# Two transformer layers on one core: the last score pairs over three PSUM tiles, a projection's tail among the first w1 groups, and w2 with the low part first

## The chip, the core and the metric

The kernel runs on one core of a Trainium2 chip. Its engines work in parallel, each through its own instruction stream: TensorE (PE, matmul; its weight loads are listed apart as PEld), VectorE (DVE), ScalarE (ACT), GpSimd (POOL) and SyncE (SP, which here only issues DMAs). Matmul results land in PSUM, eight banks of 512 fp32 columns on 128 partitions. The metric is device time in microseconds (us) of one execution; lower is better.

## The reference

Two identical layers over x of shape 1 x 2048 x 512, with the same weights in both:

```python
x = x + attention(layernorm(x), wqkv, wo)      # 32 heads of 16
x = x + mish_mlp(layernorm(x), w1, b1, w2)     # hidden 1792
x = x + attention(layernorm(x), wqkv, wo)
x = x + mish_mlp(layernorm(x), w1, b1, w2)
```

Attention is `softmax(q k^T / 4) v` over all 2048 keys, then a 512 x 512 projection wo. The MLP is `h = x w1 + b1`, `h * tanh(softplus(h))`, then w2. Everything is fp32.

## The kernel before, in words

**Precision.** Dense products (qkv, wo, w1, w2) are made from fp32r operands split in a high and a low part: `mm3` (L176) issues three matmuls per 128-row block (high x high, high x low, low x high). The p times v products are fp32.

**Tiling.** The sequence is cut in four chunks of 512 queries and sixteen key tiles of 128; heads go in eight groups of four. A *step* is one (group, chunk, key tile): 4 heads x 128 keys x 512 queries; there are 512 steps in a layer, and 16 steps make a *block*.

**Attention** needs the row maximum before the exponential. `max_mm` (L363) computes scores a first time (PSUM tag `mx`, two tiles of two banks) and DVE reduces them (L387); after 16 max steps `max_fold` (L391) folds the block's maxima, POOL splits them, and eight DMAs on SP's queue take them through DRAM (`nd`) into two extra rows of `qs`. With those rows the second computation of the scores comes out with the maximum subtracted. It is done three heads at a time: `pair` (L422) makes two heads into one two-bank tile `sp` and ACT takes the exponential (L432), `single` (L434) makes the third into a one-bank tile `ss` (L442). `pv` (L444) multiplies older p tiles with v into the accumulator `pv` (tag `acc`, one bank), and `drain` copies a finished block out. In L41 to L53, the string `CYCLE` gives the order within a step: P pair, S single, M max, v pv.

Max steps run ahead of the scores by `AHEAD` = 24 steps. The first `AHEAD + PRE` = 28 of them are put between groups of the q/k/v projections, by `some_max` in `qkv` (L538): twelve behind q/k groups and one behind every third group of three matmuls of the v projection. The first 2 x `PRE` M places of the loop go to the v projection of the last chunk (`v_parts`, L598), whose PSUM pairs share the tag `mx`. So the last 24 steps of the loop, and the four after them that hold only pv, have no maxima.

**PSUM.** Tag `mx` 2 x 2 banks, `acc` one bank, and during the loop `s2` (the pair) two banks and `s1` (the single) one: eight in all. Outside the loop the last three are three banks of tag `s`.

**After attention.** `HeadsOut` divides by the softmax sums: it loads numerators and sums from DRAM (`num`, `den`), inverts (DVE, L643), spreads the reciprocal by DMA (`rec`, POOL's queue), multiplies, and splits in `oh`, `ol`. `wo_parts` (L665) projects: sixteen groups of three matmuls a chunk, and an addition into the residual x2 (L685) after each half. In the loop's last 16 steps one group of projection 0 is issued at each step's end (`FILL`, generator `fill`). Projections 1 and 2 follow the loop, with the layer norm of chunk 0 (`norm_parts`) between their groups. Projection 3 is done in quarters within the MLP.

**MLP.** `hid(c, f)` (L690) is a w1 group of twelve matmuls and the Mish chain on ACT and DVE: hb (L701), min, exp, ..., the high part ah (L711) and then the low part al (L712). `outp(c, f)` (L715) is a w2 group of twelve matmuls into four banks; it follows `hid` by `LAG` = 2 groups, first ah with w2's two parts, then al with w2's high part. Norms of later chunks (`norm_blocks`, L266; statistics in L183) are spread over the groups by hooks.

**Buffers.** Most SBUF tiles come from the pool `blk`: 22 buffers of 8 KB per partition for everything from p tiles to weights, num, rec, oh and ol; a tile waits until a buffer comes free.

**What sets the order.** PE's order is the program's, by a chain of order-only dependencies (`pe`, L314). The other engines' instructions are ordered by a planner with a cost model, so ready work may be issued ahead of its place in the program; `behind` (L117) pins an instruction behind the one traced before it on the same engine.

Of the kernel before, what the change touches and what calls it, by code (L numbers as in the profile page):

```python
# [9 lines left out]
F32 = mybir.dt.float32  # L10
# [29 lines left out]
TR = 32  # L40
AHEAD = 24  # L41
PRE = 4
FILL = 12
KEEP = 2
# [4 lines left out]
HEADS = STEPS * HG  # L49
LAG = 2  # L50
MAX_M = (6, 3, 7)
T_BUFS = {"he": 1, "hr": 1}
# [16 lines left out]
def kernel(ctx: ExitStack, tc: tile.TileContext, x, wqkv, wo, w1, b1, w2, out):  # L69
# [113 lines left out]
    def statistics(src, nm):  # L183
        st = tmp.tile([P, NCH, 6], F32, tag="st", name=f"st{nm}")
        mv = tmp.tile([P, NCH, 2], F32, tag="mv", name=f"mv{nm}")
        ve = tmp.tile([P, NCH], F32, tag="ve", name=f"ve{nm}")
        rs = tmp.tile([P, NCH], F32, tag="rs", name=f"rs{nm}")
        for t in range(NCH):
            nc.vector.bn_stats(st[:, t], src[:, t])
            nc.vector.bn_aggr(mv[:, t], st[:, t])  # L190
        nc.gpsimd.tensor_scalar(ve, mv[:, :, 1], EPS, None, op0=ALU.add)
        nc.gpsimd.tensor_tensor(rs, ve, mhalf, op=ALU.pow)
        return rs, mv
# [110 lines left out]
    class Attention:  # L304
        def __init__(self, l, scr):
            self.l, self.scr = l, scr
            self.vscr = dram.tile([NG, P, NKT, HG * VW], F32, name=f"vscr{l}")
            self.oscr = [dram.tile([KT, 2, P, CW], F32, name=f"oscr{l}{c}") for c in range(NCH)]
            self.va = {}
            self.qk, self.mxs, self.pts, self.accs = {}, {}, [], {}  # L310
            self.singles, self.full, self.unit = 0, None, 0
            self.chained, self.last = False, None

# [49 lines left out]
        def max_mm(self, s, half):  # L363
            if s >= STEPS:
                return
            b, i = divmod(s, NKT)
# [55 lines left out]
        def pair(self):  # L422
            i = 3 * len(self.pts)
            n = min(2, HEADS - i)
            if n <= 0:
                return
            sp = self.pool.tile([P, 2, CW], F32, tag="s2", name=f"sp{self.l}{i}")
            self.pts.append(b8([P, 3, CW], F32, f"p{self.l}{i}"))
            for e in range(n):
                k, q = self.head_rows(i + e)  # L430
                self.pe(nc.tensor.matmul(sp[:, e], k, q, start=True, stop=True))  # L431
            nc.scalar.activation(self.pts[-1][:, 0:n], sp[:, 0:n], AF.Exp, scale=SCALE)  # L432
# [49 lines left out]

        def run(self, hooks, pre, fill):
            self.prep_v(0, range(NCH - 1))
            left = 2 * PRE
            close_banks()
            with tc.tile_pool(name="sa", bufs=1, space=PSUM, reuse_waits="tile") as self.pool:
                half, done = 2 * (AHEAD + PRE), -4
                for s in range(STEPS + 4):
                    if s % GSTEPS == GSTEPS - NKT and s // GSTEPS + 1 < NG:  # L490
                        self.prep_v(s // GSTEPS + 1)
                    for item in CYCLE[s % 3]:
# [15 lines left out]
                        else:  # L508
                            done += 1
                            self.pv(units(done))  # L510
                    if s + FILL >= STEPS:
                        next(fill, None)
                    for fn in hooks.get(s, []):
# [20 lines left out]
    def qkv(l, att, wts, tt, order, within, due):  # L534
# [57 lines left out]
        for c in range(NCH - 1):  # L592
            for _ in v_parts(l, c, wts, tt, att, False):
                i += 1
                if i % 3 == 0:
                    some_max()
# [68 lines left out]
    def wo_parts(l, c, outs, wot, x2, pe, paired=True):  # L665
        oh, ol = outs[c].out
        for t in range(NCH):
# [15 lines left out]
            if paired and t % 2:  # L683
                x2v = x2[:, t - 1 : t + 1]
                behind(nc.vector.tensor_tensor(x2v, acc, x2v, op=ALU.add))  # L685

    def mlp(l, x2s, w1t, w2t, tts, dst, hooks, pe):
        acts, obs = {}, {}
# [26 lines left out]
        def outp(c, f):  # L715
# [3 lines left out]
            w = w2t[f // 2]  # L719
            terms = [[(t, act, part) for t in range(NCH)] for act, part in ((ah, 0), (ah, 1), (al, 0))]  # L720
            turns = zip(*terms) if f == FT - 1 else [terms[0] + terms[1], terms[2]]
            for t, act, part in (x for turn in turns for x in turn):
                pe(
                    nc.tensor.matmul(  # L724
                        obs[c][t // 2][:, t % 2],
                        act[:, ts(t, P)],
                        w[:, part, f % 2],
                        start=f == part == 0 and act is ah,
                        stop=f == FT - 1 and act is al,
                    )  # L730
                )
# [9 lines left out]
        for i in range(len(seq) + LAG):  # L741
            if i < len(seq):
                c, f = seq[i]
                hid(c, f)
                for fn in hooks.get((c, f), []):
                    fn()
# [50 lines left out]
    for l in range(2):  # L797
# [58 lines left out]

        fill = project(0)
        att.run(hooks, v_parts(l, NCH - 1, wts, tt, att, True), fill)
        outs[3].load()
# [39 lines left out]
        if l == 0:  # L899
            last = NCH - 1  # L900
            for f, js in ((2, (0,)), (4, (2,)), (9, (1,)), (11, (3,)), (12, (4,)), (13, (5,))):
                hooks.setdefault((last, f), []).append(lambda js=js: load_qkv(1, wts, js, splits))
            for c in range(last):
                spread(hooks, last, (1, 5, 8)[c], x2s[c], f"q1{c}", tt, c)
        mlp(l, x2s, w1t, w2t, tts, xs if l == 0 else out, hooks, att.pe)
    close_banks()

# [27 lines left out]
```

## Time and profile before

| | us |
|---|---|
| median of 3 runs | 3534.33 (3533.1 to 3535.59) |
| the profiled execution | 3532.86 |
| its span | 3531.1 |
| PE busy | 3512.9 (99%) |
| DVE busy | 3002.7 (85%) |
| ACT busy | 2582.8 (73%) |
| POOL busy | 239.2 (7%) |

The profile is of one execution; its times are us from the first instruction. Rows of a timeline read: start, duration, engine, line, operation, output<-input tiles, shape (for PE rows x columns of the weights, then the output), count, and in brackets how long the engine sat idle before and what released it. Names drop buffer numbers: `mo` is a w2 accumulator, `h` a w1 one, `wo`, `va`, `vp` those of the projections, `pm` the scores for the maxima. The ends of matmuls are modelled: a stretched matmul can hide a wait. The granted clock of TensorE (PEclk) is 0.999 over the run.

### The profile page before, as it was taken

To read this page: it belongs to the slowest core of one execution; us is meant where nothing else is said; L and a number is where in the kernel's file an instruction comes from. 1 tells how busy PE (TensorE), PEld (TensorE's weight loads), DVE (VectorE), ACT (ScalarE), POOL (GpSimd) and SP (SyncE) were. 2 spreads that over 40 slices of the span, in tenths; PEclk is the share of its full clock that TensorE was granted. 3 is DMA by queue.
4 is the path that set the end of the run, shared out by engine and by line. 5 is a ranking of instruction groups with operands and counts; after the bars stand their busy time and mean duration, and the time that the engine had idled before them with its cause. 6 is when DMAs were issued, how large, how long until landed. Compare 5 with 4: busy or idle time off the path is not lost.

```text
span 3531.1 us, 68820 instructions
## 1 busy us (share of the span) xinstructions
PE 3512.9 (99%) x28572; PEld 1922.5 (54%) x28572; DVE 3002.7 (85%) x3160; ACT 2582.8 (73%) x3513; POOL 239.2 (7%) x392
## 2 busy tenths in 40 slices
PE   9999999999999999999999999999999999999999
PEld 7644444444444444788876444444444444447887
DVE  6789999999999994776756999999999999947665
ACT  3288888888888888356622888888888888874665
POOL 3100001010000002100010000000000000021000
PEclk9999999999999999999999999999999999999999
DMA  7641312213131124630364211112121111247100
GB/s 250 228 92 47 83 47 74 61 51 71 43 81 42 49 81 71 207 96 25 111 217 147 48 39 38 38 29 44 31 36 39 41 36 31 79 74 222 66 13 24
DMA packets 182196, 273.97 MB, mean 78 GB/s; under 512 B 67508, under 2 KB 111476, under 8 KB 168060
## 3 DMA queue, kind: packets, MB, share of 16 engines
q1 hardware_dynamic: 154964, 192.91, 21.4%
q10 hardware_dynamic: 19176, 43.06, 3.5%
q0 software_dynamic: 7744, 33.60, 3.4%
q8 instruction: 224, 3.67, 0.4%
q14 instruction: 88, 0.72, 0.1%
HBM read 158.87 MB, written 109.58 MB: 76 GB/s over the span
## 4 chain that ended last, share of the span: by engine, by line
PE 96%; DVE 2%; DMA 1%; issue 1%; ACT 0%; POOL 0%; SPq 0%; DVEq 0%; ACTq 0%; POOLq 0%
PE pv L457 30%; PE pm L383 18%; PE ss L441 13%; PE sp L431 10%; PE mo L724 8%; PE h L179 3%; PE h L181 3%; PE h L180 3%; PE qk L179 2%; PE qk L180 1%; PE qk L181 1%; PE wo L179 1%; PE va L179 1%; PE wo L181 1%; PE wo L180 1%
## 5 line engine op out<-in xcount | busy, mean ns | idle before, releaser
L387 DVE TENSOR_REDUCE mxv<-pm 128x2 f32<-128x1024 f32 x2048 | 2385.2, 1219 | 138.6 <-PE pm L383 88.5
L432 ACT ACTIVATE p<-sp 128x1024 f32<-128x1024 f32 x1366 | 1395.9, 1022 | 19.7 <-PE sp L431 15.3
L457 PE MATMUL pv<-p,va 128*32 128x256 f32 (+2 forms) x16032 | 1166.9, 392 | 0.1
L383 PE MATMUL pm<-ks,qs 48*128 48x512 f32 x4096 | 1096.0, 446 | 0.3
L442 ACT ACTIVATE p<-ss 128x512 f32<-128x512 f32 x1364 | 814.6, 597 | 349.1 <-PE ss L441 263.5
L431 PE MATMUL sp<-qs,ks 50*128 50x512 f32 x2732 | 725.6, 447 | 0.5 <-ACT p L432 0.2
L457 PEld LDWEIGHTS pv<-p,va 128*32 128x32 f32 x16032 | 367.7, 108 | 498.4 <-issue 420.6
L383 PEld LDWEIGHTS pm<-ks,qs 48*128 48x128 f32 x4096 | 449.9, 184 | 345.6 <-issue 216.6
L441 PE MATMUL ss<-qs,ks 50*128 50x512 f32 x1364 | 611.0, 448 | 0.0
L441 PEld LDWEIGHTS ss<-qs,ks 50*128 50x128 f32 x1364 | 252.0, 185 | 329.5 <-ACT p L442 225.5
L431 PEld LDWEIGHTS sp<-qs,ks 50*128 50x128 f32 x2732 | 261.1, 183 | 200.5 <-ACT p L432 119.1
L402 POOL CAST np<-nt 128x32 fp32r<-128x32 f32 x64 | 13.3, 208 | 2213.4 <-DVE nt L400 2213.4
L701 ACT ACTIVATE hb<-h,b1t 128x512 f32<-128x512 f32 x112 | 76.7, 685 | 96.6 <-PE h L181 90.6
L173 ACT ACTIVATE pt<-qk 128x512 fp32r<-128x512 f32 x64 | 38.2, 597 | 143.5 <-PE qk L181 102.9
L705 ACT ACTIVATE hr<-he 128x512 f32<-128x512 f32 x112 | 70.9, 633 | 82.3 <-DVE he L704 82.3
L708 DVE TENSOR_TENSOR hb<-hb,hr 128x512 f32<-128x512 f32 x112 | 77.2, 689 | 51.0 <-ACT hr L706 49.3
L712 DVE TENSOR_TENSOR al<-hb,ah 128x512 fp32r<-128x512 f32 x112 | 77.2, 690 | 36.8 <-ACT ah L711 33.8
L711 ACT ACTIVATE ah<-hb 128x512 fp32r<-128x512 f32 x112 | 70.5, 629 | 50.7 <-DVE hb L708 40.1
L702 DVE TENSOR_SCALAR he<-hb 128x512 f32<-128x512 f32 x112 | 47.5, 424 | 67.0 <-ACT hb L701 61.6
L704 DVE SCALAR_TENSOR_TENSOR he<-he 128x512 f32<-128x512 f32 x112 | 77.0, 687 | 25.4 <-ACT he L703 24.8
L703 ACT ACTIVATE he<-he 128x512 f32<-128x512 f32 x112 | 70.3, 628 | 32.2 <-DVE he L702 32.2
L174 DVE TENSOR_TENSOR pt<-qk,pt 128x512 fp32r<-128x512 f32 x64 | 43.9, 686 | 52.8 <-ACT pt L173 50.7
(235 smaller groups left out, 3081.8 us busy)
## 6 DMA issues: line engine op xcount, KB each, us to landing
scr<-pt ACTq DMA_DIRECT2D x64, 512.0 KB
qs<-scr SPq DMA_DIRECT2D x174, 128.0 KB
ks<-scr SPq DMA_DIRECT2D x174, 128.0 KB
vscr<-v SPq DMA_DIRECT2D x32, 512.0 KB
va<-vscr SPq DMA_DIRECT2D x64, 256.0 KB
oscr<-ot SPq DMA_DIRECT2D x64, 256.0 KB
ww<-sw POOLq DMA_DIRECT2D x14, 1024.0 KB, 4.9
num<-oscr SPq DMA_DIRECT2D x64, 128.0 KB
```

The costliest lines, as they stand in the source:

```text
L179: pe(nc.tensor.matmul(acc, ah, bh, start=first and i == 0, stop=False))
L180: pe(nc.tensor.matmul(acc, ah, bl, start=False, stop=False))
L181: pe(nc.tensor.matmul(acc, al, bh, start=False, stop=last and i == n - 1))
L383: nc.tensor.matmul(pm[:, e], qs[u][rows, q0 : q0 + P], ks[u][rows, ts(n, 512)], start=True, stop=True)
L387: nc.vector.tensor_reduce(self.mxs[b][:, 2 * u : 2 * u + 2, qt, n], pm, axis=AX.X, op=ALU.max)
L431: self.pe(nc.tensor.matmul(sp[:, e], k, q, start=True, stop=True))
L432: nc.scalar.activation(self.pts[-1][:, 0:n], sp[:, 0:n], AF.Exp, scale=SCALE)
L441: self.pe(nc.tensor.matmul(sp, k, q, start=True, stop=True))
L442: nc.scalar.activation(self.pts[i // 3][:, 2], sp, AF.Exp, scale=SCALE)
L457: nc.tensor.matmul(self.accs[b][ts(h, VW), cols], self.va[b // NCH][:, kt, h, :], self.pts[j][:, e, cols], start=kt == 0 and q0 == 0, stop ...
L708: nc.vector.tensor_tensor(hb, hb, r, op=ALU.mult)
L724: nc.tensor.matmul(obs[c][t // 2][:, t % 2], act[:, ts(t, P)], w[:, part, f % 2], start=f == part == 0 and act is ah, stop=f == FT - 1 and ...
```

## The change

- `AHEAD` goes from 24 to 22. The number of max steps before the loop becomes 26, and in the v projection they come at `i % 3 == 1` instead of `i % 3 == 0`.
- `FILL` is gone. Projection 0 is issued whole after the loop.
- Once `max_mm` finds no more max steps (`idle`), two of three score pairs take a tile of the tag `mx` and the third the tile `s2`.
- Projection 2 is split: `HEAD` = 10 of its 16 groups are issued as before, three groups behind the first w1 group, and the remaining three behind the second. Its halves' additions into x2 (c = 2) are no longer pinned.
- The statistics of `norm_blocks` are pinned behind the DVE instruction traced before them.
- A w2 group takes al with w2's high part first, then ah with the high part, then ah with the low part.

```diff
-AHEAD = 24
+AHEAD = 22
-FILL = 12
+HEAD = 10
@@ statistics
-            nc.vector.bn_stats(st[:, t], src[:, t])
-            nc.vector.bn_aggr(mv[:, t], st[:, t])
+            behind(nc.vector.bn_stats(st[:, t], src[:, t]))
+            behind(nc.vector.bn_aggr(mv[:, t], st[:, t]))
@@ max_mm
             if s >= STEPS:
+                self.idle = self.idle or 1
                 return
@@ pair
-            sp = self.pool.tile([P, 2, CW], F32, tag="s2", name=f"sp{self.l}{i}")
+            spare = self.idle and self.idle % 3
+            self.idle += self.idle > 0
+            pool, tag = (ps, "mx") if spare else (self.pool, "s2")
+            sp = pool.tile([P, 2, CW], F32, tag=tag, name=f"sp{self.l}{i}")
@@ run
-                    if s + FILL >= STEPS:
-                        next(fill, None)
@@ qkv
-                if i % 3 == 0:
+                if i % 3 == 1:
                     some_max()
@@ wo_parts
-                behind(nc.vector.tensor_tensor(x2v, acc, x2v, op=ALU.add))
+                ins = nc.vector.tensor_tensor(x2v, acc, x2v, op=ALU.add)
+                if c < 2:
+                    behind(ins)
@@ mlp
-            terms = [[(t, act, part) for t in range(NCH)] for act, part in ((ah, 0), (ah, 1), (al, 0))]
-            turns = zip(*terms) if f == FT - 1 else [terms[0] + terms[1], terms[2]]
+            terms = [[(t, act, part) for t in range(NCH)] for act, part in ((al, 0), (ah, 0), (ah, 1))]
+            turns = zip(*terms) if f == FT - 1 else terms
...
-                        start=f == part == 0 and act is ah,
-                        stop=f == FT - 1 and act is al,
+                        start=f == 0 and act is al,
+                        stop=f == FT - 1 and part == 1,
...
                 hid(c, f)
+                for _ in range(3 + i):
+                    next(rest, None)
@@ the layer
-        fill = project(0)
-        att.run(hooks, v_parts(l, NCH - 1, wts, tt, att, True), fill)
+        att.run(hooks, v_parts(l, NCH - 1, wts, tt, att, True))
...
-        for _ in fill:
+        for _ in project(0):
             pass
...
-        for i, _ in enumerate(project(2)):
+        last = project(2)
+        for i in range(HEAD):
+            next(last)
...
-        mlp(l, x2s, w1t, w2t, tts, xs if l == 0 else out, hooks, att.pe)
+        mlp(l, x2s, w1t, w2t, tts, xs if l == 0 else out, hooks, att.pe, last)
```

More of the change, by code (lines that the diff above doesn't have):

```diff
@@ L311, in __init__ @@
             self.singles, self.full, self.unit = 0, None, 0
+            self.idle = 0
             self.chained, self.last = False, None
@@ L481, in drain, with run @@
             nc.sync.dma_start(self.oscr[qb][g // 2, g % 2], ot)
-        def run(self, hooks, pre, fill):
+        def run(self, hooks, pre):
             self.prep_v(0, range(NCH - 1))
@@ L684, in wo_parts, with mlp @@
                 x2v = x2[:, t - 1 : t + 1]
-                behind(nc.vector.tensor_tensor(x2v, acc, x2v, op=ALU.add))
-    def mlp(l, x2s, w1t, w2t, tts, dst, hooks, pe):
+                ins = nc.vector.tensor_tensor(x2v, acc, x2v, op=ALU.add)
+                if c < 2:
+                    behind(ins)
+    def mlp(l, x2s, w1t, w2t, tts, dst, hooks, pe, rest):
         acts, obs = {}, {}
@@ L899 @@
         if l == 0:
-            last = NCH - 1
+            end = NCH - 1
             for f, js in ((2, (0,)), (4, (2,)), (9, (1,)), (11, (3,)), (12, (4,)), (13, (5,))):
-                hooks.setdefault((last, f), []).append(lambda js=js: load_qkv(1, wts, js, splits))
-            for c in range(last):
-                spread(hooks, last, (1, 5, 8)[c], x2s[c], f"q1{c}", tt, c)
-        mlp(l, x2s, w1t, w2t, tts, xs if l == 0 else out, hooks, att.pe)
+                hooks.setdefault((end, f), []).append(lambda js=js: load_qkv(1, wts, js, splits))
+            for c in range(end):
+                spread(hooks, end, (1, 5, 8)[c], x2s[c], f"q1{c}", tt, c)
+        mlp(l, x2s, w1t, w2t, tts, xs if l == 0 else out, hooks, att.pe, last)
     close_banks()
```

## The prediction

> **What bounds the kernel now.** I read the page first: the engine totals, then the chain that ended last.
>
> ```profile
> span 3531.1 us, 68820 instructions
> PE 3512.9 (99%) x28572; PEld 1922.5 (54%) x28572; DVE 3002.7 (85%) x3160; ACT 2582.8 (73%) x3513; POOL 239.2 (7%) x392
> PE 96%; DVE 2%; DMA 1%; issue 1%; ACT 0%; POOL 0%; SPq 0%; DVEq 0%; ACTq 0%; POOLq 0%
> ```
>
> PE is the chain, but its 99% is modelled: a matmul that starts late still counts as busy if the one before it is stretched over the gap. So idle time has to be read from the starts of neighbouring matmuls. For that I cut layer 0 into stretches: three attention blocks (48 loop steps), the 24 steps at the end that have scores but no maxima, the four steps with pv alone, and the one stretch with a low clock.
>
> ```profile
> core 0: us, PE busy (x) PEld busy (x) DVE busy (x) ACT busy (x) POOL busy (x), PEclk, DMA share, GB/s
> 1003.96:1119.99 116.03, 116.03 (x1140) 52.61 (x1142) 112.34 (x102) 99.55 (x132) 9.29 (x12) 1.00 0.18 50
> 1350.61:1412.60 61.99, 61.80 (x494) 25.14 (x490) 15.81 (x12) 49.61 (x65) 22.44 (x40) 1.00 0.49 78
> 1412.60:1419.43 6.83, 6.83 (x62) 3.23 (x61) 3.20 (x2) 1.79 (x3) 1.90 (x1) 1.00 0.01 2
> 1455.23:1458.65 3.42, 3.42 (x10) 2.65 (x9) 3.02 (x6) 2.65 (x5) 0.00 (x0) 0.50 1.14 164
> ```
>
> A step with maxima costs 116.03 / 48 = 2.42 us. The tail then takes 61.99 + 6.83 = 68.8 us. I call single scores, pair, pv one slot; four slots make three steps. In the timeline of the tail, PE rows and one ACT row:
>
> ```profile
> 1360.61 0.49 PE L441 MATMUL ss<-qs,ks 50*128 50x512 f32 x1
> 1361.08 0.50 PE L431 MATMUL sp<-qs,ks 50*128 50x512 f32 x2
> 1361.51 0.86 PE L457 MATMUL pv<-p,va 128*32 128x128 f32 x16
> 1362.30 0.49 PE L441 MATMUL ss<-qs,ks 50*128 50x512 f32 x1
> 1360.00 1.02 ACT L432 ACTIVATE p<-sp 128x1024 f32<-128x1024 f32 x1
> ```
>
> The slot is 1362.30 - 1360.61 = 1.69 us (1.675 over many). The pair's matmuls start at 1361.08, just after the exp of the previous pair ends (1361.02), although the single was issued 0.47 earlier: there is one pair tile, so exp 1.02, matmuls about 0.5 and two hand-overs form a closed loop of 1.675.
>
> **The change part by part.** (1) *Three pair tiles.* What remains is PE's own order or ACT's. Rows of the same tail where the pair tile happened to be free, and ACT rows of a block's end, where it had work waiting:
>
> ```profile
> 1405.18 0.50 PE L441 MATMUL ss<-qs,ks 50*128 50x512 f32 x1
> 1405.18 0.73 PE L431 MATMUL sp<-qs,ks 50*128 50x512 f32 x2
> 1405.84 0.86 PE L457 MATMUL pv<-p,va 128*32 128x256 f32 x16
> ...
> 1337.27 1.02 ACT L432 ACTIVATE p<-sp 128x1024 f32<-128x1024 f32 x1
> 1338.19 0.59 ACT L480 ACTIVATE ot<-pv 128x512 f32<-128x512 f32 x1
> 1338.66 0.60 ACT L442 ACTIVATE p<-ss 128x512 f32<-128x512 f32 x1
> ```
>
> Single and pair together take 0.66 on PE, and pv 0.79 (1361.51 to 1362.30): 1.45. ACT gives way after 0.92 (pair) and 0.47 to 0.5 (512 columns): about 1.40. So the new slot is 1.45, PE's, between 1.45 and the 1.675 of now; I take 1.45 because both engines have shown that rate.
>
> (2) *Projection 0 leaves the tail.* Its 16 groups of three matmuls sat between the slots:
>
> ```profile
> 1413.38 0.50 PE L179 MATMUL wo<-wo1l,oh 128*128 128x512 f32 x1
> 1414.28 0.86 PE L457 MATMUL pv<-p,va 128*32 128x256 f32 x16
> ...
> 1513.69 2.80 PE mo L724 x12
> ```
>
> A group between pv's takes 0.90 (1413.38 to 1414.28); twelve in a row of their own kind take 2.80, so 0.70 for three and 11.0 for projection 0 behind the loop. New tail, counted from the same step: two steps that now still have maxima (AHEAD 22) 2 x 2.42 = 4.84; 22 steps = 29.33 slots x 1.45 = 42.5; four slots of pv alone 4 x 0.79 = 3.2, with 0.2 for the last hand-over of the accumulator; projection 11.0: 61.7, so 7.1 less in each layer.
>
> A cost stands against it. The 22 buffers of `blk` are shared by the p tiles and by num, rec, oh, ol of three chunks, which come from a chain of fixed length: fold, reciprocal, POOL's DMAs, product, ol.
>
> ```profile
> 1351.62 0.22 DVE L396 TENSOR_REDUCE folded<-mxv 128x16 f32<-128x64 f32 x1
> 1356.89 1.14 SPq L409 DMA_DIRECT2D qs<-nd  x4
> 1375.11 2.29 DVE L662 TENSOR_TENSOR ol<-num,oh 128x2048 fp32r<-128x2048 f32 x1 [5.28 <-POOL oh L659]
> ...
> POOL oh L659 <- PE pv L457: 15.8, 2, 8.8
> ```
>
> The first ol ends 25.8 us after the fold (last row, a view of the waits: POOL already waits for buffers that pv frees). Now the fold is 4.84 later while the steps behind it shrink from 2.23 to 1.93, so ol ends at about 1382.2 and step 501, which asks for the next oh and ol, comes at 1376.7: 5.5 us with three or four p tiles instead of five. The trace does not show what p tiles cost then: between 0 and all of the gain on slots, 29.33 x 0.23 = 6.7. I take 2.0, a third of the 5.5, since four tiles nearly suffice. Net -5.1 per layer.
>
> (3) *AHEAD 22* takes two max steps from the v projection and sets the rest two thirds of a group earlier (i % 3 == 1).
>
> ```profile
> 115.41 0.73 PE L383 MATMUL pm<-ks,qs 48*128 48x512 f32 x4
> 124.61 0.73 PE L383 MATMUL pm<-ks,qs 48*128 48x512 f32 x4
> 127.54 0.50 PE L383 MATMUL pm<-ks,qs 48*128 48x512 f32 x2
> 117.69 3.56 DVE L387 TENSOR_REDUCE mxv<-pm 128x2 f32<-128x1024 f32 x3
> 164.56 0.50 PE L179 MATMUL vp<-sqkv,thq 128*128 128x512 f32 x1 [0.86 <-DVE mxv L387]
> ```
>
> Max step to max step is 2.93; nine va matmuls of it are 9 x 0.233 = 2.10, so one costs 0.83: -1.7 for two. The wait of 0.86 at the loop's start, where the first v pair needs the tile of the last maximum, goes. But the first max step now follows its predecessor (115.41) after three matmuls, at about 117.0, while DVE frees the second tile only after the first of the three reduces, at 117.69 + 1.2 = 118.9: PE goes on at 119.3 instead of 117.6, so it loses 1.7. Today's first one loses 0.4 by the same rows (it comes at 118.35 after nine matmuls), so +1.3. Net -1.3 per layer (-1.7 - 0.86 + 1.3). The lead of a block's fold over its first score shrinks by two steps to 6 x 2.42 less the 1.0 from step to fold = 13.5 us; fold to the last issue of qs is 6.4, and qs waited at most 1.6 for nd's landing, so about 8.1 are needed. For the last block, 8 slots x 1.45 less 1.0 = 10.6. I cost it at nothing.
>
> (4) *Tail of projection 2 behind the first w1 groups.* PE rows at the start of both MLPs:
>
> ```profile
> 1454.90 3.52 PE L724 MATMUL mo<-w20l,ah 128*128 128x512 f32 x8 [2.16 <-ACT ah L711]
> 1458.22 1.30 PE L724 MATMUL mo<-w20l,al 128*128 128x512 f32 x4
> 1474.78 2.12 PE L724 MATMUL mo<-w21l,ah 128*128 128x512 f32 x8 [1.41 <-ACT ah L711]
> 3211.17 1.20 PE L724 MATMUL mo<-w20l,ah 128*128 128x512 f32 x4 [2.16 <-ACT ah L711]
> 3228.08 2.13 PE L724 MATMUL mo<-w21l,ah 128*128 128x512 f32 x8
> 3230.55 1.20 PE L724 MATMUL mo<-w21l,al 128*128 128x512 f32 x4 [0.35 <-DVE al L712]
> ...
> 3517.64 0.69 ACT L701 ACTIVATE hb<-h,b1t 128x512 f32<-128x512 f32 x1
> 3523.07 0.69 DVE L712 TENSOR_TENSOR al<-hb,ah 128x512 fp32r<-128x512 f32 x1 [0.76 <-ACT ah L711]
> ```
>
> The first w2 group waits 2.16 in both layers; in layer 0 half the clock follows (the last stretch above), and eight matmuls last 3.32 (1454.90 to 1458.22) instead of 8 x 2.80 / 12 = 1.87: 3.6 in layer 0, 2.2 in layer 1. Eighteen matmuls, 4.1 us, now stand between. Undisturbed, hb to the end of al is 6.1 (last two rows), and the time from the first w1 group's end to the first w2 group becomes 9.5: 3.4 to spare, even with al first. The six groups are moved past two loads on SP's queue (w1, w2 blocks two and one), which are then traced earlier; nothing of theirs is needed for 20 us. Both waits go.
>
> [...]
>
> (5) *Statistics pinned in program order, the last add unpinned.* Now two chunks' statistics, scalings and transposes sit among the first MLP groups; pinned, they start at group 7. The second wait (1.4 in layer 0 by the row at 1474.78; 0.6 in layer 1, where the eight at 3228.08 last 2.47) lies behind them and behind num and ol (4.6 of DVE, which stay): I leave 0.5 of each, so -0.9 and -0.1. Their cover: from group 7 to the next chunk is 7 x 5.5 = 39 us (a w1 and a w2 group, 24 matmuls, are 5.6), for some ten DVE instructions under 1 us each, POOL's two and two rounds of DMA. Without it, PE would stall at the chunk's start. And at the first transposes
>
> ```profile
> 1428.82 0.66 PE L256 MATMUL tpm<-ident,xnm 128*128 128x128 f32 x4 [0.37 <-DVE xnm L210]
> ```
>
> 0.4 goes in each layer, because two early statistics on DVE stand before xnm.
>
> (6) *Low part first* costs where al is late: at the kernel's end two matmuls that ran ahead of al now follow it, +0.4 once (layer 0's end is filled by the next layer's q and k). Elsewhere al is 3 us early.
>
> Sum: layer 0: -5.1 - 1.3 - 3.6 - 0.9 - 0.4 = -11.3. Layer 1: -5.1 - 1.3 - 2.2 - 0.1 - 0.4 + 0.4 = -8.7. From the profiled 3532.86 (1.8 over its span): 3512.9. The median of the runs is 1.5 above the profiled one, so 3514.
>
> **The rivals.** *The rotation does not lift the slot* (p tiles, or the order of ACT): the tail's -5.1 goes in both layers, 3524. For it: the full `blk`. Against it: three tiles break the loop of 1.675 whatever else holds. *The first w2 wait comes back*, because ACT takes the second hb before the first exp, as it does now, and al goes first: 5.8 and 1.0 stay, 3521. Against it: 3.4 to spare. *Both*: 3531, no change. *Slower: the lead of the fold is too short.* All 62 later blocks would stall on PE by what fold to qs exceeds 13.5. That eats the gain of 20 at 0.32 each and is slower by 7 from 0.44, a latency of 13.9 against 8.1 now; at 14.5 the time is 3514 + 62 = 3576. It would need SP or POOL held for 6 us in every block. *The clock*: a stretch of half clock in the tail, as in the row at 1455.23, costs 1.7 per 3.42 us; if every second one in the 42.5 us were so, 10.6 a layer, 3535. The tail now waits in every slot at clock 1.00, which speaks against it. [...]
>
> **How the numbers follow.** Forecast 0.56, slot 0.20, w2 wait 0.12, both 0.05, fold 0.05, clock 0.02. A measurement of this kernel tells 0.2%, 7 us, from no change. Faster 0.56 + 0.20 + 0.12 = 0.88; same 0.05; slower 0.07. The range goes down to 3503 (no p-tile cost, no second wait, some us of unseen order) and up to 3528, over the two partial cases.
>
> **What would show it.** Slots of 1.45 between ss starts in the tail and clock 1.00; projection 0 in one run of 11 us; no pause before the first mo; va groups without maxima at the end of the v projection; no wait of ss on the fold at a block's start. I am wrong if slots stay at 1.6 or more, if mo waits for al, or if PE pauses every 16 steps.

## The result: 0.6% slower

| | before | changed |
|---|---|---|
| median | 3534.96 us (3533.1 to 3535.61) | 3552.62 us (3551.5 to 3563.09) |
| ratio to before | | 1.0057, 95% interval 1.0038 to 1.0077 |
| span of the profiled execution | 3531.1 | 3551.1 |

The forecast was 3514, range 3503 to 3528. The first lines of the changed kernel's page (span, engine totals, chain of waits):

```profile
span 3551.1 us, 68757 instructions
PE 3514.0 (99%) x28572; PEld 1931.2 (54%) x28572; DVE 3004.5 (85%) x3160; ACT 2580.2 (73%) x3513; POOL 242.3 (7%) x392
PE 93%; DMA 2%; DVE 2%; issue 1%; ACT 1%; POOL 1%; SPq 0%; DVEq 0%; ACTq 0%; POOLq 0%
```

The engine totals are nearly those of before (PE 3514.0 against 3512.9); of these lines the span and the chain tell that PE has lost time, 93% of the chain instead of 96%. Which waits these are stands in the list of what PE waited for (us in total, times, longest us):

```profile
PE ss L446 <- ACT p L447: 14.2, 4, 6.1
PE mo L729 <- DVE al L717: 10.4, 6, 3.7
PE pm L385 <- DVE mxv L389: 2.8, 4, 1.2
```

Before, none of the three came to more than 0.3 us. The longest entry of that list then is gone:

```profile
PE mo L724 <- ACT ah L711: 5.7, 3, 2.2
```

The stretches of the changed kernel, by start and end, then length, busy times, granted clock, DMA share, GB/s; first three blocks of the loop, then the tail of layer 0 (last max step to last pv) and in it the stretch of half clock, the last MLP chunk of layer 0, the v projection of layer 0, the tail of layer 1:

```profile
1013.44:1129.50 116.06, 116.06 (x1138) 52.61 (x1136) 112.27 (x103) 99.43 (x132) 9.26 (x12) 1.00 0.16 47
1359.24:1422.44 63.20, 55.97 (x484) 21.02 (x481) 16.87 (x13) 44.84 (x62) 24.35 (x41) 0.78 0.50 77
1395.50:1419.40 23.90, 20.73 (x122) 7.20 (x122) 4.43 (x3) 14.49 (x19) 6.05 (x12) 0.50 0.53 75
1708.74:1799.20 90.46, 83.15 (x346) 66.71 (x345) 70.20 (x131) 47.40 (x77) 5.94 (x6) 0.96 0.47 155
116.38:166.35 49.97, 48.55 (x202) 31.80 (x200) 36.18 (x33) 6.62 (x12) 12.62 (x13) 0.93 0.56 179
3131.07:3185.92 54.85, 47.45 (x484) 18.74 (x481) 14.00 (x11) 44.32 (x62) 22.45 (x40) 0.94 0.56 88
```

The last MLP chunk of layer 0 before, for comparison:

```profile
1699.75:1779.23 79.48, 79.48 (x344) 64.44 (x343) 56.90 (x99) 46.97 (x77) 1.62 (x2) 1.00 0.47 159
```

DVE has 131 entries and 70.2 us of work there now, 99 and 56.9 before; POOL has 6 instead of 2. I cut both layers into stretches by the starts of the matmuls that begin them, and set the forecast's own terms beside them (us; "repaired" is the last experiment, e12):

| stretch | L0 before | forecast | changed | repaired | L1 before | forecast | changed | repaired |
|---|---|---|---|---|---|---|---|---|
| v projection | 47.2 | 46.8 | 50.0 | 45.8 | 47.2 | 46.8 | 47.1 | 45.8 |
| loop to last max step | 1186.2 | 1190.2 | 1192.9 | 1192.8 | 1186.7 | 1190.7 | 1192.5 | 1192.6 |
| last max step to last pv | 68.6 | 47.9 | 63.2 | 45.5 | 68.6 | 47.9 | 54.8 | 45.4 |
| last pv to first w1 group | 26.3 | 32.8 | 31.3 | 31.2 | 26.3 | 32.8 | 31.2 | 31.2 |
| to first w2 group | 10.5 | 12.4 | 12.9 | 12.9 | 10.5 | 12.4 | 12.9 | 12.9 |
| first MLP chunk | 89.0 | 86.6 | 86.7 | 85.6 | 86.6 | 86.5 | 87.5 | 86.2 |
| second and third | 155.9 | 155.9 | 155.5 | 155.5 | 155.6 | 155.6 | 155.5 | 155.5 |
| last chunk | 79.5 | 79.5 | 90.5 | 83.3 | 72.7 | 73.1 | 73.1 | 72.7 |

Of the prediction's term (3), -1.7 and +1.3 fall in the v projection; the wait of 0.86 stood in the loop's first step and is counted there. Against the forecast, layer 0 lost 15.3 in the tail, 11.0 in the last chunk, 3.1 in the v projection and 2.7 in the loop; layer 1 lost 6.9 in the tail, 1.9 in the loop and 0.3 in the v projection. From the last pv to the end of the third chunk, taken together, layer 0 came out 1.3 better than forecast and layer 1 0.2.

**The tail.** Its first third runs as forecast (timeline of the changed kernel, PE):

```profile
1360.59 0.49 PE L446 MATMUL ss<-qs,ks 50*128 50x512 f32 x1
1362.03 0.49 PE L446 MATMUL ss<-qs,ks 50*128 50x512 f32 x1
```

1362.03 - 1360.59 = 1.44: the slot forecast at 1.45. Some 31 us after these it stops (timeline; PE, DVE and ACT):

```profile
1391.24 0.50 PE L446 MATMUL ss<-qs,ks 50*128 50x512 f32 x1
1394.73 2.29 DVE L665 TENSOR_TENSOR ol<-num,oh 128x2048 fp32r<-128x2048 f32 x1 [2.13 <-POOL oh L662]
1397.11 1.02 ACT L437 ACTIVATE p<-sp 128x1024 f32<-128x1024 f32 x1 [6.09 <-DMA num<-oscr]
1398.67 0.79 PE L446 MATMUL ss<-qs,ks 50*128 50x512 f32 x1 [5.92 <-ACT p L447]
1401.26 0.79 PE L446 MATMUL ss<-qs,ks 50*128 50x512 f32 x1
```

The same wait in layer 1 (DVE and ACT):

```profile
3165.32 2.29 DVE L665 TENSOR_TENSOR ol<-num,oh 128x2048 fp32r<-128x2048 f32 x1 [2.13 <-POOL oh L662]
3167.69 1.02 ACT L437 ACTIVATE p<-sp 128x1024 f32<-128x1024 f32 x1 [6.18 <-DVE ol L665]
```

The exponential stands still for 6.09 until `ol` of chunk 1 ends (1394.73 + 2.29 = 1397.02): `ol` is the last reader of num, and with it a buffer comes free for a p tile. (Layer 0's row names a load of num, layer 1's names `ol`; in both, `ol` ended less than 0.1 before.) PE waits 5.92 for the exponential, and comes back at half the clock: the next slot takes 1401.26 - 1398.67 = 2.59. So layer 0's tail lost 6.0 in the pause; 1.2 in a smaller one some 12 us earlier, where an exponential waits for `num` of chunk 0, and about 1.5 in the 3.4 us of half clock behind that one; and 9.1 in eight slots of 2.59, 1.14 extra each: 17.8. That is, to within 0.5, the 15.3 over the forecast and the 2.0 that the forecast had set aside. Where the 36 us between fold and `ol` go (timeline of the changed kernel, DVE and POOL):

```profile
1361.05 0.22 DVE L398 TENSOR_REDUCE folded<-mxv 128x16 f32<-128x64 f32 x1
1361.58 1.76 DVE L646 RECIPROCAL den<-den 128x128 f32<-128x128 f32 x2
1377.08 2.29 DVE L658 TENSOR_TENSOR num<-num,rec 128x2048 f32<-128x2048 f32 x1 [13.74 <-DMA rscr<-den]
1379.38 4.05 POOL L654 DMA_DIRECT2D rec<-rscr  x8 [5.35 <-PE sp L436]
1390.31 2.29 DVE L658 TENSOR_TENSOR num<-num,rec 128x2048 f32<-128x2048 f32 x1 [2.65 <-DMA rec<-rscr]
```

Both reciprocals follow the last fold. From chunk 0's reciprocal through memory to its product it is 15.5 (1361.58 to 1377.08), chunk 1's spread starts on POOL at 1379.38, just as that product ends (1379.37), and its `ol` ends at 1397. Before, the same work took about as long, 34.4 from the fold's end (1351.84) to the end of this row of `ol` for chunk 1:

```profile
1383.98 2.29 DVE L662 TENSOR_TENSOR ol<-num,oh 128x2048 fp32r<-128x2048 f32 x1 [2.14 <-POOL oh L659]
```

But the tail was longer then, 62.7 from the last max step to the last pair where the forecast has 42.5, and used p tiles more slowly.

**The last chunk of layer 0.** Rows of the timeline around its longest pauses:

```profile
1748.87 1.00 DVE L278 TENSOR_SCALAR xnq<-x,mvq,rsq 128x512 f32<-128x512 f32 x2 [0.93 <-POOL rsq L192]
1753.69 0.68 DVE L717 TENSOR_TENSOR al<-hb,ah 128x512 fp32r<-128x512 f32 x1
1754.43 2.07 PE L729 MATMUL mo<-w23l,al 128*128 128x512 f32 x4 [3.67 <-DVE al L717]
1787.69 2.19 ACT L294 ACTIVATE thq<-tlq 128x512 fp32r<-128x512 f32 x4 [6.84 <-DMA tlq<-ntq]
```

Layer 1's first norm stands in this chunk, its statistics now pinned there, and `al`, which a w2 group now needs first, comes behind them on DVE.

**The v projection.** The second max step waits as forecast (1.73 for its second half), but the clock is halved from 118.9 for 6.8 us (timeline, PE):

```profile
117.53 0.50 PE L385 MATMUL pm<-ks,qs 48*128 48x512 f32 x2 [0.19 <-DVE mxv L389]
119.26 0.80 PE L385 MATMUL pm<-ks,qs 48*128 48x512 f32 x2 [1.23 <-DVE mxv L389]
```

### The profile page after: what moved, and what is told of

Same layout as the page of the kernel before. It is cut to its first block, busy times and chain, and to the rows that moved or that the text cites. A ratio compares the mean times of both kernels' runs of the same rounds, so it can differ in the third digit from the quotient of the medians.

```text
span 3551.1 us, 68757 instructions
## 1 busy us (share of the span) xinstructions
PE 3514.0 (99%) x28572; PEld 1931.2 (54%) x28572; DVE 3004.5 (85%) x3160; ACT 2580.2 (73%) x3513; POOL 242.3 (7%) x392
## 4 chain that ended last, share of the span: by engine, by line
PE 93%; DMA 2%; DVE 2%; issue 1%; ACT 1%; POOL 1%; SPq 0%; DVEq 0%; ACTq 0%; POOLq 0%
PE pv L462 30%; PE pm L385 18%; PE ss L446 13%; PE sp L436 9%; PE mo L729 7%; PE h L181 2%; PE h L179 2%; PE h L180 2%; PE qk L179 2%; PE qk L180 1%; PE qk L181 1%; PE va L179 1%; PE wo L179 1%; PE wo L181 1%; PE wo L180 1%
## 5 line engine op out<-in xcount | busy, mean ns | idle before, releaser
L436 PE MATMUL sp<-qs,ks 50*128 50x512 f32 x2732 | 743.7, 446 | 0.5 <-ACT p L437 0.4
L436 PEld LDWEIGHTS sp<-qs,ks 50*128 50x128 f32 x2732 | 271.5, 184 | 185.1 <-ACT p L437 112.4
L710 ACT ACTIVATE hr<-he 128x512 f32<-128x512 f32 x112 | 70.8, 632 | 91.4 <-DVE he L709 91.3
```

## The experiments

The theory after the comparison: the tail's pause is the buffers', held by a chain of fixed length that the shorter tail runs into; the rest is half clock after pauses, and DVE's order in the last chunk. The rival for the tail is that three tiles in turn by themselves lower the clock or stall PE. Kernels with half clock in them scatter between executions by up to 13 us (e9: 3536.25 to 3548.95), so the stretches decide as much as the medians. All are edits of the changed kernel; ratios are to the kernel before.

**e1_late: the chains of chunks 1 and 2 asked for later.** The four numbers are steps before the end at which a chunk's load, reciprocal, spread, and product with split are traced.

```diff
-(-42,-20,-19,-13), (-26,-19,-18,-11), (-10,-6,-4,0)
+(-42,-20,-19,-13), (-10, -6, -5,  0), ( -4, 0, 2,3)
```

> The changed kernel, with chunks 1 and 2 of num, rec, oh and ol asked for later (loads at steps -10 and -4 from the end instead of -26 and -10, the rest after them), so that fewer of the 22 buffers are taken while score pairs still need p tiles. Theory buffers: the pause of 6 us that the changed kernel shows in the middle of the tail (1391.9 to 1398.7 in layer 0) is an exponential that waits for a p tile until ol has freed num and rec; without it there is no pause, every slot is 1.45, the clock stays at 1.00 in the tail, and the tail of layer 0 (last maximum to last pair) goes from 60.5 to 43, that of layer 1 from 52.1 to 43: 3552 - 17 - 9 = about 3526. Rival clock by bank cycling: it is the turn over three PSUM tiles itself that lets the clock fall; then stretches at half clock stay in the tail without a pause before them, and the time stays above 3540. Rival chain: projections 1 and 2 now wait for their oh and ol instead, a new pause between the projections, and no more than half of the gain.

3603.44 us, ratio 1.0197 (1.0180 to 1.0214). Its stretches (columns as above): the tail of layer 0 to the last pair, the one of layer 1, a stretch of projection 1, and what follows it:

```profile
1358.58:1401.19 42.61, 42.41 (x436) 16.63 (x433) 8.60 (x8) 42.32 (x60) 14.54 (x27) 1.00 0.60 92
3150.66:3193.32 42.66, 42.46 (x436) 16.64 (x433) 8.61 (x8) 42.45 (x60) 14.53 (x27) 1.00 0.59 90
1415.24:1453.86 38.62, 0.39 (x3) 0.03 (x1) 8.51 (x6) 0.00 (x0) 7.97 (x13) 0.57 0.97 264
1453.86:1458.30 4.44, 4.44 (x11) 3.47 (x12) 4.04 (x9) 0.00 (x0) 0.16 (x1) 0.50 0.01 4
```

And the two rows of its timeline that end the long stretch:

```profile
1445.99 2.29 DVE L658 TENSOR_TENSOR num<-num,rec 128x2048 f32<-128x2048 f32 x1 [28.11 <-DMA rec<-rscr]
1453.86 0.76 PE L179 MATMUL wo<-wo0l,oh 128*128 128x512 f32 x1 [38.23 <-DVE x L688]
```

With the buffers free, the tail is 42.6 in both layers, at clock 1.00: the forecast's 42.5 for 29.33 slots. So three tiles in turn by themselves neither stall PE nor lower its clock in this tail, and the rival falls. The chain itself has not gone away: DVE waits for it at `num` with the residual additions behind, and PE waits 38 us for those.

**e2_norot: all pairs in one tile again, the rest as changed.**

```diff
-            spare = self.idle and self.idle % 3
+            spare = 0
```

> The changed kernel, with all score pairs in the one tile s2 as before (the rest of the change stays, projection 0 behind the loop too). Theory buffers: slots go back to 1.675, the buffers are asked for more slowly, so the pause shrinks to 0 to 3 us and the clock does not fall; the tail (22 steps, 29.3 slots) is 49 to 52 in both layers instead of 60.5 and 52.1, so 3540 to 3552, layer 0 faster than the changed kernel by about 10, layer 1 the same. Rival clock by bank cycling: half clock goes and the pause of 6 stays, tail 55 to 57 in both. If the rotation itself were a gain whatever else happens, this run would be slower than the changed kernel by 6 in each layer.

3556.72, ratio 1.0062 (1.0047 to 1.0077). The tails to the last pair are 56.8 and 58.5; with the slower slot there is still a pause at the same place, 33 us behind the last max step, of 5.1 and 4.1, with half clock behind it for 6.8 and 13.7. So the pause doesn't need the rotation. With the slow slot it is enough that projection 0 is gone from the tail: e6, next, has the same 22 steps and the same one tile, with projection 0 put back, and no pause.

**e6_fill: one pair tile and projection 0 among the last 12 steps and the four behind them, as before; the rest as changed (AHEAD 22 too).**

```diff
-            spare = self.idle and self.idle % 3
+            spare = 0
...
+                    if s + FILL >= STEPS:
+                        next(fill, None)
```

> The changed kernel with its tail as before: pairs in one tile, and projection 0 among the last 12 steps of the loop. If the pause in the tail comes because its cover (projection 0 and two steps) was taken away, it is gone here: from the last maxima to the last pv 58 and 6 us, first w1 group 27 us later, no half clock, so the tail is worth -3.5 us in layer 0 and +5 in layer 1 against the changed kernel as profiled, 3551 to 3554 in all. If the three tiles had been a gain in spite of the pause, the time is above 3556; if they and the moved projection are what made the kernel slower, it is below 3545.

3558.81, ratio 1.0066 (1.0051 to 1.0081). From the last max step to the last pv 65.9 and 65.1, at full clock, no pause in the tail. But the first w1 group now comes 21.7 behind the last pv instead of 31.2, and the time is lost there (DVE and PE rows of the first chunk):

```profile
1472.89 2.29 DVE L661 TENSOR_TENSOR num<-num,rec 128x2048 f32<-128x2048 f32 x1 [6.76 <-DMA rec<-rscr]
...
1484.23 2.07 PE L732 MATMUL mo<-w21l,al 128*128 128x512 f32 x4 [7.62 <-DVE al L720]
```

Chunk 3's chain, 47.6 us from the last pv (1425.29) to `num`, holds DVE, and a w2 group waits 7.6 for `al`; the first chunks take 95.6 and 94.9 instead of 86.7 and 87.5. So moving projection 0 behind the loop paid for part of what moving projection 2's tail takes away as cover: this chain, too, ran beside work that the change makes shorter or moves. The expected 3551 to 3554 had left it out.

**e3_unpin: statistics not pinned anywhere**, and **e10_qun: pinned only within the MLP, not for layer 1's first norm.**

```diff
-            behind(nc.vector.bn_stats(st[:, t], src[:, t]))
-            behind(nc.vector.bn_aggr(mv[:, t], st[:, t]))
+            nc.vector.bn_stats(st[:, t], src[:, t])          # e10: pinned where the norm's
+            nc.vector.bn_aggr(mv[:, t], st[:, t])            # name begins with "m"
```

> The changed kernel, with the statistics of norm_blocks free to be issued early again. Theory pins: the 10.5 us that layer 0 lost in its last MLP chunk (90.5 instead of 79.5 from w2 end to w2 end, with three pauses and half clock after two of them) come from the next layer's norms, which pinned statistics set late among the Mish chain, so that DVE and then ACT wait in order for POOL and for the DMA of the transposed chunk; unpinned, the chunk is back at 79 to 82, the time 3541 to 3545, and the start of the MLPs loses 1 to 2 again. Rival low first: the pauses come from w2 groups that wait for al; then the chunk stays at 87 or more.

> The changed kernel with the statistics pinned only for the norms inside the MLP, not for those of layer 1's first norm, which lie in the last MLP chunk of layer 0. If the pins are what holds DVE up there, that chunk falls from 90.5 us to 80 to 83, the first chunks stay at 86.7 and 87.5, and the time is 3542 to 3546. If the low part first is enough to stall that chunk by itself, it stays above 86 and the time is 3548 to 3553.

3555.73, ratio 1.0059 (1.0044 to 1.0074), and 3553.79, ratio 1.0053 (1.0038 to 1.0068): no gain in either. Without any pins the last chunk of layer 0 falls from 90.5 to 82.4, but the first chunks go from 86.7 and 87.5 to 91.4 and 91.3. With pins in the MLP alone (e10), the third and the last chunk of layer 0 as stretches:

```profile
1623.33:1709.09 85.76, 81.52 (x337) 65.29 (x336) 66.74 (x126) 46.53 (x74) 4.79 (x6) 0.96 0.22 62
1709.09:1792.29 83.20, 80.68 (x348) 65.13 (x347) 57.28 (x100) 47.01 (x77) 1.62 (x2) 1.00 0.45 152
```

The same statistics have gone one chunk ahead (126 groups on DVE there, 100 in the last) and stall that one: 169.0 together, 168.2 with all pins. The expectation of 3542 to 3546 for e10 was wrong: the stall moved with the statistics. It doesn't take the low part first for that: e11, with the same pins and the high part first, still has 83.1 in the third chunk, where all pins give 77.7.

**e4_ahfirst: the high part first again in w2.**

```diff
-            terms = [... for act, part in ((al, 0), (ah, 0), (ah, 1))]
+            terms = [... for act, part in ((ah, 0), (ah, 1), (al, 0))]
```

> The changed kernel, with w2 groups in the old order (ah with both parts of w2, then al). Theory pins: the pauses in layer 0's last chunk get shorter by what al lags ah (1.2 to 1.9 each, three of them), not more, so that chunk is 85 to 88 instead of 90.5; the second wait of layer 1's MLP shrinks from 1.8 to about 0.7, and the kernel's end gains 0.4: 3545 to 3549 in all. Rival low first: the chunk goes back to 80, 3541 or less.

3545.07, ratio 1.0030 (1.0018 to 1.0042), 7.5 below the changed kernel. The stretch of the last chunk of layer 0 is

```profile
1702.92:1784.39 81.47, 78.24 (x336) 62.78 (x335) 65.50 (x124) 44.75 (x74) 5.83 (x6) 1.00 0.48 155
```

9.0 shorter, at full clock; the first chunks take 85.6 and 85.9, 1.0 and 1.6 less, and the kernel's end 0.5. So the low part first, costed at 0.4, costs about 12 between these two profiles. The changed kernel's 90.5 is the longest of its kind, though. The seven profiles with all pins and the low part first have 86.5 to 90.5 there, 87.6 in the mean; the three with all pins and the high part first (e4, e7, e12) 81.5 to 84.0, 82.9 in the mean. With 4.7 for the last chunk the order costs between 7 and 8, as the medians say.

**e8_third: the v projection's max steps where they were.**

```diff
-                if i % 3 == 1:
+                if i % 3 == 0:
```

> The changed kernel with the maxima steps of the v projection where they were (after every third va group from the start). Forecast was that the shift costs 1.3 at the first step, and with AHEAD 22 in both this kernel gives that back: the v projection's stretch 46 to 47 us instead of 50.0 in layer 0 (no half clock there) and 46.5 instead of 47.1 in layer 1, the time 3549 to 3552. If the half clock at 119 us came from something else, the stretch in layer 0 stays at 50 and the time at 3552.6.

3544.51, ratio 1.0026 (1.0016 to 1.0035), better than the 3549 expected. The v projection takes 45.77 in both layers, at full clock (the stretch of layer 0):

```profile
117.24:163.01 45.77, 45.66 (x203) 30.11 (x201) 36.26 (x33) 6.62 (x12) 12.68 (x13) 1.00 0.63 203
```

That is 4.2 and 1.4 less than in the changed kernel. The shift, with its 1.7 us wait at the second max step, which the forecast had costed as 1.7, is what lets the half clock in: all nine profiled kernels with `i % 3 == 1` have a half-clock stretch of 3.4 or 6.8 us in the v projection of one of the layers, and none of the four changed ones with `i % 3 == 0` has one. The wait itself stands in both layers each time, and only one of them gets the half clock. The rest of the 8 us of medians is not located: tails and last chunks of the two profiles differ by several us both ways.

**e5_buf: chunk 1's spread asked for 7 steps later, its product and split 11; chunk 2's one.**

```diff
-(-26,-19,-18,-11), (-10,-6,-4,0)
+(-26,-19,-11,  0), (-10,-6,-4,1)
```

> The changed kernel, with the product and split of chunk 1's sums asked for seven and eleven steps later, and the last split of chunk 2 one step later: fewer shared buffers are held by them while the last exponentials run. If the pause in the tail is made by exponentials that wait for a shared buffer, the stretch from the last maxima to the last score pair falls from 60.5 and 52.1 us to 42 to 45 in both layers, with no half clock in it, projection 1 starts without a wait, and the time comes to about 3527 (3552.6 less 17 and 9). If the buffers have no part in it, the pause stays at about 5 us and the time stays within 5 us of 3552.6. If the split is now too late for projection 1, a pause appears behind the last pv instead and the time lies between.

3548.02, ratio 1.0039 (1.0024 to 1.0054); the pause is there, later and longer: it begins 35.1 us behind the last max step and lasts 8.6 and 9.4. The tails to the last pair are 54.7 and 55.5. In this kernel (ACT row) the exponential waits for another end of the chain:

```profile
1399.10 1.02 ACT L437 ACTIVATE p<-sp 128x1024 f32<-128x1024 f32 x1 [8.88 <-DVE num L658]
```

The product of num and rec, after which rec's buffer is free, ended 0.1 before it. So the reading behind this run, that the buffers are asked for too soon, was half of it: what counts is when the chain gives them back, and asking later makes that later. **e7_besta**, the same with the high part first and `i % 3 == 0`:

> The changed kernel with three repairs: the later split of chunks 1 and 2, the high part first again in the w2 blocks, and a maxima step after every third va group from the start on as before. If the losses are those of the buffers (about -25), of the low part (about -8) and of the v projection's first maxima (-1 to -3), the time is 3515, at least 10 below the kernel before. If the half clock finds another place to start, the time is 3525 to 3540.

3536.57, ratio 1.0002 (0.9992 to 1.0011): level with before, 21.6 above what was hoped; its tails still take 55.9 and 55.3.

**e9_early: chunk 0's reciprocal and spread 14 steps earlier, its product 7.** This turns the edit round.

```diff
-(-42,-20,-19,-13), (-26,-19,-18,-11), (-10,-6,-4,0)
+(-42,-34,-33,-20), (-26,-19,-18,-10), (-10,-6,-4,1)
```

> The changed kernel with one table of steps altered: chunk 0's reciprocal is taken 14 steps earlier, inside the last full blocks, its product and split 7 steps earlier, chunk 1's chain follows it. Theory: the pause in the tail is made by a chain of fixed length (reciprocal, a round through memory, product, split, about 36 us behind the last fold for two chunks in a row) that now ends while exponentials still need its buffers. Then half of the chain lies in front of the last fold, two buffers more are free from 7 us after it, and the tail from the last maxima to the last score pair falls from 60.5 and 52.1 us to 43 to 46 with no half clock: 3552.6 less 17 and 8 is 3528. The rival, that three tiles in turn lower the clock or that the pause comes from PE or ACT themselves, expects the pause of 5 us or more to stay, and 3545 to 3556.

3540.75, ratio 1.0018 (1.0009 to 1.0028), 12 below the changed kernel but short of 3528. The pause now begins 26.4 and 26.5 us behind the last max step instead of 33.5 and 32.0, and has shrunk to 3.5 and 2.3; the tails to the last pair are 49.2 and 49.5. The chain of chunk 1 in layer 0 (DVE, ACT), and PE's pause in layer 1:

```profile
1359.24 0.22 DVE L398 TENSOR_REDUCE folded<-mxv 128x16 f32<-128x64 f32 x1
1367.02 0.95 DVE L646 RECIPROCAL den<-den 128x128 f32<-128x128 f32 x1
1383.42 2.29 DVE L658 TENSOR_TENSOR num<-num,rec 128x2048 f32<-128x2048 f32 x1 [15.45 <-DMA rec<-rscr]
1385.79 1.02 ACT L437 ACTIVATE p<-sp 128x1024 f32<-128x1024 f32 x1 [3.73 <-DVE num L658]
...
3145.68 0.79 PE L446 MATMUL ss<-qs,ks 50*128 50x512 f32 x1 [2.31 <-ACT p L447]
```

The exponential starts 0.08 after `num` ends, and chunk 1's reciprocal stands behind chunk 0's product and split, 7.6 us behind the fold's end (1359.46 to 1367.02), where in the changed kernel it followed at once. **e11_win** is e9 with the high part first, `i % 3 == 0` and e10's pins:

> All repairs together: chunk 0's chain early, the high part first again in the w2 blocks, the v projection's maxima after every third group from the start on, and the statistics of layer 1's first norm unpinned. If the tail is 43 to 46 us without half clock in both layers (-10 each against the kernel with the later split, 3536.6) and the last chunk of layer 0 goes from 84 to 80.5, the time is 3513, some 22 below the kernel before. If the half clock finds another place to start, it is 3520 to 3536.

3528.98, ratio 0.9984 (0.9975 to 0.9994): below before, with pauses of 3 us and half clock for 6.8 and 13.7 in the tails, as its second case had it.

**e12_first: chunk 1's round ahead of chunk 0's product**, with the high part first, `i % 3 == 0`, all pins.

```diff
-(-42,-34,-33,-20), (-26,-19,-18,-10), (-10,-6,-4,1)
+(-42,-34,-33,-18), (-26,-20,-19,-10), (-10,-6,-4,1)
```

> As in the last run, but with chunk 1's reciprocal and round through memory traced ahead of chunk 0's product and split, and with all statistics pinned as in the changed kernel. There an exponential waited until the product of chunk 1 set its reciprocals free, and that product came 15 us behind the reciprocal, which stood behind 7.4 us of chunk 0's work on DVE. If the lateness of that chain is all that pauses the tail, it ends 6 to 7 us sooner here, more than the pause of 2.4 to 3.5, and the tail is 42.6 to 44 us at full clock in both layers; with the last chunk of layer 0 as with all pins (77.8 and 84 us for the last two chunks against 83.1 and 80.3), the time is 3529 less 6, 8 and 2: 3513. If the pause only moves to the next chain (chunk 2's), a pause stays behind 30 us and the time is 3522 to 3530.

3511.47 (3510.22 to 3512.22), ratio 0.9937 (0.9921 to 0.9954): faster than both kernels. The stretches of both tails (last max step to last pv) and of the last chunk of layer 0:

```profile
1356.14:1401.61 45.47, 45.21 (x484) 18.02 (x481) 13.04 (x10) 43.81 (x62) 16.37 (x28) 1.00 0.52 82
3101.28:3146.68 45.40, 45.20 (x483) 18.01 (x481) 13.04 (x10) 44.17 (x62) 16.35 (x28) 1.00 0.51 82
1686.83:1770.13 83.30, 80.07 (x344) 64.27 (x343) 66.64 (x126) 45.92 (x76) 5.81 (x6) 1.00 0.50 161
```

Its fold and its product of chunk 1 (timeline, DVE):

```profile
1357.95 0.22 DVE L398 TENSOR_REDUCE folded<-mxv 128x16 f32<-128x64 f32 x1
1374.38 2.29 DVE L658 TENSOR_TENSOR num<-num,rec 128x2048 f32<-128x2048 f32 x1 [2.06 <-DMA rec<-rscr]
```

The fold ends at 1358.17, the product at 1376.67: 18.5 behind it, 26.3 in e9. No pause is left in either tail; half clock stands only in the last 4.3 us of the kernel. The tails hold the same rotation, the same steps and the same 22 buffers as the changed kernel's; what differs there is when and in which order the chains are asked for. From e11, which still pauses, this kernel differs only in that order and in the pins of layer 1's first norm.

## Why the prediction was wrong

By its own steps:

- **(1) Three pair tiles: right.** Slot 1.44 in the changed kernel where nothing stops it, 42.6 to 42.7 for 29.33 slots in e1 and e12, full clock.
- **(2) Projection 0 behind the loop, p-tile cost 2.0: this is the step that failed.** The mechanism was in it (buffers, `ol` 25.8 after the fold, 5.5 us with three or four tiles), but it followed one chunk's chain. The second chunk's runs behind the first's and ends 36 us after the fold, 37.8 behind the last max step. Before, it ended at about the same distance, 36.8, but the last pair came at 62.7; in the forecast the last pair comes at 42.5. Priced at 2.0 and bounded by 6.7, because I took scarce buffers as a slower slot, it was 17 in layer 0 and 9 in layer 1: a full stop of some 6 us, and half clock behind it. A bound made of "all of the gain on slots" is no bound for a stop. The runs for it are e1 (later: tail right, pause elsewhere), e9 and e12 (earlier: pause shrinks, then goes).
- **(3) AHEAD 22: right in the wait of 1.7 at the second max step, wrong in stopping there.** With that wait the clock fell in one layer or the other; for the v projection -0.4 a layer was forecast (-1.7 and +1.3), and the changed kernel shows +2.7 and -0.1. e8 and e12, without the shift, show -1.5: where the clock held, the shift costs 1.4 against the 1.3 forecast. The wait of 0.86 is gone. The fold's lead was enough, as costed. The loop took 1.9 to 2.7 more than the two steps less that wait; part of it lies in the first three blocks, and 0.1 to 0.2 in most groups of three after them. Its cause stays open.
- **(4) Projection 2's tail: right.** The waits at the first w2 groups are gone, and the first w1 to the first w2 group takes 12.9 where 12.4 was forecast. But its cover was not named: in e6, where projection 0 is back in the loop, the moved groups leave chunk 3's chain 9.5 us less, and 7.6 come back.
- **(5) Pinned statistics: right for the chunks it looked at, and it looked at too few.** The first chunk of layer 0 came out at 86.7 against 86.6, in part by luck: 1.0 of the 86.7 is the low part's (85.6 in e4), for which nothing was set down there. Layer 1's first norm uses the same function in layer 0's last chunk, and was not counted.
- **(6) Low part first, +0.4: mis-sized.** At the kernel's end it is 0.5. "Elsewhere al is 3 us early" does not hold in the first chunks, which lose 1.0 and 1.6 by it, and still less in the last chunk of layer 0, where norms share DVE: there `al` is late, and with the pins the order cost 9 against e4, 4.7 in the mean of the kernels.

The sum was otherwise sound. Without the p-tile term, the 0.4 of (6) and the 1.3 of the shift in (3) it gives -14.6 for layer 0 and -12.4 for layer 1. Counted to the end of each layer, e12, which has none of the three, stands at -9.1 and -11.8. Of the 5.5 that layer 0 lacks, 3.8 are its last chunk, 83.3 against 79.5 with the statistics pinned there, and 1.5 lie ahead of the v projection, whose start differs by up to 2.6 between the profiles.

Of the rivals, *the rotation does not lift the slot* named the buffers but not a stop. *The clock* was the nearest, with half clock in the tail and 3535. Half clock came, but behind a pause and not by the three tiles taken in turn: e1 and e12 take them in turn at clock 1.00, and e2, which doesn't, has half clock behind its pause. The prediction argued against the clock because "the tail now waits in every slot at clock 1.00"; those waits are parts of a us each, and say nothing of one stop of 6.

## What to carry to other kernels

When a stretch of PE gets shorter, list every chain of fixed length that runs beside it (here: reciprocal, round through memory, product, split) with its end counted from the same event, for each chunk in turn since they queue on the same engines, and see which of them now ends later than the stretch. What was short of buffers here did not slow down, it stopped; give the buffers back earlier by ordering the chain, not by asking for them later. And an operand needed first must be early in every place where the code runs, the one with the busiest engine above all.

## What was not expected of the hardware

Half clock came after short pauses, and it stayed long. A PE pause of 2.31 in e9's layer 1 (the row at 3145.68) was followed by 10.2 us of granted clock 0.5, one of 1.2 to 1.7 in the v projection by 3.4 or 6.8, one of 5.9 in the changed kernel by 23.9 that began within it, although PE was in use through most of that stretch (20.7 of 23.9). Not every short pause did it: those of 0.9 to 1.4 in the tails of e4 and e8 passed at full clock, and of the two of 2.16 before the first w2 groups of the kernel before, layer 0's was followed by 3.4 us at 0.50 and layer 1's by none (clock 1.00 from 3208 to 3222). In e1's projection 1, a dense run of matmuls, the clock was back 4.4 us after the pause ended (0.50 from 1453.86 to 1458.3), but in the tail, where each slot has small pv matmuls and a wait, the half clock lasted 3.4 to 23.9 us, and not the same from layer to layer or from kernel to kernel. It goes with the scatter of the kernels with pauses: of the changed kernel's four executions the shortest, 3551.5, has a mean granted clock of 0.995 and the longest, 3563.09, 0.991. What sets the length, and which pause brings it, no run here shows.
